# First layer: lower words of the weights made on VectorE in one operation, sums added from PSUM by VectorE, and GpSimd's paired operations merged

## The chip, the cores and the metric

The kernel runs on one core of a Trainium2 chip. The metric is the device time of one execution in microseconds (us), median of three runs. In the rows, PE is TensorE's matmuls, PEld its weight loads, DVE is VectorE, ACT is ScalarE, POOL is GpSimd and SP is SyncE, which issues the transfers.

## The reference

Eight batches of 576 tokens with 8 heads of 64 go through an attention over 32 memory slots per head, and the result (4608 tokens of width 512) goes through two feed-forward layers of width 2048. All is float32; the weights are drawn as float64 and reach the kernel as pairs of 32-bit words.

```python
a = np.exp(phi - np.max(phi, axis=2, keepdims=True))        # per head: 32 slots
a = a / (np.sum(a, axis=2, keepdims=True) + 1e-09)
k_m = np.einsum('bhsm,bhsd->bhmd', a, k)
v_m = np.einsum('bhsm,bhsd->bhmd', a, v)
scores = np.matmul(q, k_m.transpose(0, 1, 3, 2)) / np.sqrt(64)
attn = softmax(scores)                                      # over the 32 slots
x = np.matmul(attn, v_m)                                    # -> 4608 x 512
h = x @ moe_w_in;  x = np.where(h > 0, h, np.exp(np.minimum(h, 0)) - 1) @ moe_w_out
h = x @ moe2_w_in; return (h * np.clip(h + 3, 0, 6) / 6) @ moe2_w_out
```

## The kernel before, in words

Precision is kept by splitting every operand of a large product into a high part `hi` that the matrix engine takes exactly and a rest `lo`; each product is three matmuls (hi hi, hi lo, lo hi).

**First layer.** The tokens are 16 units of 288 (`T`). The attention's second product is folded into the weights `w_in` (`fold`, tiles `pw` and `wf`), so that PE makes the hidden values of one unit and one chunk of 128 hidden channels straight from the attention weights `ahi`/`alo`: this is `first(n)`, six matmuls into the PSUM tile `ph`. `middle(n)` turns `ph` into `e` and then into `g` (high and low): two operations on ACT (L671, L673), one on DVE (L675), a cast on ACT (L680) and the subtraction that leaves the low part on POOL (L682). `second(n)` multiplies `g` with the chunk of `w_out` into four PSUM tiles `acc0` to `acc3`, twelve matmuls (L706). There are 256 such items n. The first four units are worked in four quarters of the hidden channels (q = 0 to 3; quarter, then unit, then chunk), so that the weights can be made while they are used; the sums of a quarter are kept in SBUF tiles `st`, and after each later quarter `leave` adds the new sums to them. 16 blocks of four items end so, 12 of them with an addition. The other twelve units run through all 16 chunks at once.

**The weights.** `convert` makes float32 weights from the two 32-bit words of a float64. `raw` holds both words. From the upper word come the float without the lowest bits (L284 on ACT, L289, L291, L294 on DVE) and its power of two (L297 on DVE, into the place of the upper word). The lower word is scaled by 2^-52 on ACT (L287), multiplied with that power of two on POOL (L310, one operation for each chunk of 512) and added on DVE (L312). A piece is a pair of chunks, 128 x 1024; the first two pairs are worked in halves of 512. For `w_out` (`how` is "parts") a cast on ACT (L317) and a subtraction on POOL (L321) follow and give the `w1o` tiles. For the second layer's weights (`how` is "seven") the scaling and the multiplication are one DVE operation already (L300), and L303 is the addition. 16 pairs belong to the first layer, 16 to the second.

**Order.** All instructions stand in an order that a planner writes down when the program is built: each piece of work is a generator that yields a `Piece` with an engine, an estimated cost, what it needs and which buffers it takes; lanes of pieces compete by due times, and the engines' queues are filled in the planned order. Each engine then works its queue strictly in that order and waits where something is not ready. The estimated costs thus decide only the order; `early=READ` makes a piece compete as if it were due 12 items sooner.

**Second layer.** From about 720 us on, five blocks of tokens go through a scheme of seven products each; the change does not touch it.

Of the kernel before, what the change touches and what calls it, by code (L numbers as in the profile page):

```python
# [21 lines left out]
P = 128  # L22
T = 288
# [74 lines left out]
class Schedule:  # L98
# [17 lines left out]
    def mark(self, *key):  # L116
        self.done[key] = self.end

    def give(self, name, n=1):
        self.slots[name] += [self.end] * n  # L120
# [60 lines left out]
def mixer(ctx, tc, phi_t, phi_n, kv, q_t, w1i, w1o, w2i, w2o, out):  # L181
# [25 lines left out]
    def new(kind, shape, name, dt=F32):  # L207

        return pools[kind].tile(shape, dt, tag=kind, name=name)
# [34 lines left out]
    def drop(n, c):  # L244

        dropped[n] = dropped.get(n, 0) + c.stop - c.start
        if dropped[n] == 2:
            give("blk" if n in INTO else "raw")
            if n in INTO:
                give("pair")  # L250
# [14 lines left out]
    def convert(n, c, name, i, f, how, *keys):  # L265
# [19 lines left out]
        if how != "seven":  # L285
            yield Piece("act", 0.2 + 0.43 * m)
            act.activation(out=rest, in_=low, func=ACTF.Copy, scale=2.0 ** -52)  # L287
# [9 lines left out]
        dve.tensor_scalar(high, topu, 0xFF800000, None, op0=ALU.bitwise_and)  # L297
        if how == "seven":
            yield Piece("dve", two)
            dve.scalar_tensor_tensor(out=rest, in0=low, scalar=2.0 ** -52, in1=highf,  # L300
                                     op0=ALU.mult, op1=ALU.mult)
            yield Piece("dve", two)
            dve.tensor_tensor(out=top, in0=top, in1=rest, op=ALU.add)  # L303
            drop(n, c)
            tops[name, (i * FQ + f) // 2] = top
            mark("top", name, (i * FQ + f) // 2)
            return
        for x in range(m):
            yield Piece("pool", 1.2)
            pool.tensor_tensor(out=rest[:, x], in0=rest[:, x], in1=highf[:, x], op=ALU.mult)  # L310
        yield Piece("dve", two)
        dve.tensor_tensor(out=top, in0=top, in1=rest, op=ALU.add)  # L312
        drop(n, c)
        if how == "parts":
            yield Piece("act", 0.2 + 0.43 * m, **made(name, i, f, 2))
            hi, lo = make(name, i, f, m, "hl")
            act.copy(hi, top)  # L317
        for x in range(m):
            if how == "parts":
                yield Piece("pool", 1.4)  # L320
                pool.tensor_tensor(out=lo[:, x], in0=top[:, x], in1=hi[:, x].bitcast(F32),  # L321
                                   op=ALU.subtract)
            mark(name, i, f + x)
# [236 lines left out]
    def softmax(b, hf, pss, a):  # L560
# [31 lines left out]
        act.copy(a[0], zt)  # L592
        for g in range(NG):
            yield Piece("pool", 0.85)
            pool.tensor_tensor(out=a[1][:, g], in0=zt[:, g], in1=a[0][:, g].bitcast(F32),  # L595
                               op=ALU.subtract)
            mark("a", b, hf, g)
# [90 lines left out]
    def second(n):  # L688
# [4 lines left out]
        keys = [("acc", count - 1, i) for i in range(2)] if begin and count else []  # L693
# [9 lines left out]
        if close:  # L703
            passes.sort(key=lambda p: p[0])
# [11 lines left out]
    def leave(n, u, part, acc, count, i):  # L716

        key = ("second", n) if i == 0 or part else ("st", count)
        first, last = part in (None, 0), part in (None, NQ - 1)
        kind = "xy"[u >= YST]  # L720
        for d in range(i, KD, 2):
            slots = (kind, kind, "ta"[u >= YST], "ta"[u >= YST]) if (
                first and (i, d) == (0, 0)) else ()
            if not first and i == 0:
                slots = ("e",)
            engine = "act" if i == 0 or part == 0 else "dve"
            yield Piece(engine, 0.36, key, slots=slots)
            if kind in slots:
                sums2[u] = [new(kind, [P, 2, T], "st") for _ in range(2)]
                mark("st", count)  # L730
                mark("sums", u)
            st = sums2[u][d // 2][:, d % 2]
            if first and engine == "dve":
                dve.tensor_copy(st, acc[d])
            elif first:
                act.copy(st, acc[d])
            elif i:
                dve.tensor_tensor(out=st, in0=st, in1=acc[d], op=ALU.add)
            else:
                e = new("e", [P, T], "e")  # L740
                act.copy(e, acc[d])
                adds.add(add(st, d, e, count), due=n + 8)
            if n == n2 - 1:
                give(f"acc{d}")
        mark("acc", count, i)
        if last and i == 0:
            for j in range(2):
                keys = [("acc", count, 0), ("acc", count, 1)]
                if part:
                    keys += [("add", count, 2 * j)]  # L750
                leave2.add(finish(u, j, keys), due=n)

    def add(st, d, e, count):
        yield Piece("pool", 0.75)
        pool.tensor_tensor(out=st, in0=st, in1=e, op=ALU.add)
        give("e")
        mark("add", count, d)
# [268 lines left out]
    adds, leave2 = sch.lane(), sch.lane()  # L1026
# [174 lines left out]
```

## Time and profile before

| | |
|---|---|
| median of three runs | 1463.32 us (1461.45 to 1464.34) |
| the profiled execution | 1463.72 us |
| its span, first to last instruction | 1461.9 us |
| PE busy | 1414.6 us (97%) |
| DVE busy | 1095.0 us (75%) |
| ACT busy | 817.2 us (56%) |
| POOL busy | 458.8 us (31%) |

The span and the profiled execution's own time differ by 1.8 us, which lie before the first and after the last instruction. Busy shares over the whole span mix stages: POOL's 31% is nearly all in the first 700 us. An instruction counts as busy from its start to its end, so what it waits inside for a memory port is in its duration.

### The profile page before, as it was taken

The numbers are of one execution on the slowest core, as the hardware profiler recorded it, in microseconds if no ns is written. First come the engines' busy times: TensorE is split into PE (matmuls) and PEld (weight loads), VectorE is DVE, ScalarE is ACT, GpSimd is POOL, SyncE is SP. The second block draws the span as 40 slices with busy tenths as digits, with TensorE's granted clock in tenths as the row PEclk, the third lists the DMA queues.
The fourth block names the chain that finished last, engine by engine and source line by source line (L and its number), as shares of the span: only waits on it lengthen the run. The fifth ranks groups of instructions, "written<-read, shape, count | busy, mean of one in ns | idle before, by whom it ended". The sixth has DMA issues, their size and how long they took to land.

```text
span 1461.9 us, 25619 instructions
## 1 busy us (share of the span) xinstructions
PE 1414.6 (97%) x9464; PEld 1283.9 (88%) x9464; DVE 1095.0 (75%) x1785; ACT 817.2 (56%) x1691; POOL 458.8 (31%) x464
## 2 busy tenths in 40 slices
PE   4698999999999999999999999999999999999999
PEld 2588898989999899999998888888888888889998
DVE  5998865677586786767357896789678867986785
ACT  4677775667667676667653454355335534553453
POOL 1678984456557565656420000000000000000000
PEclk7799999999999999999999999999999999999999
DMA  9421215336546455654336468556936783676562
GB/s 363 184 80 71 102 63 178 101 112 236 174 162 204 155 180 178 200 170 167 124 111 239 170 226 338 194 182 222 370 140 209 247 352 131 210 274 270 204 234 117
DMA packets 94221, 279.41 MB, mean 191 GB/s; under 512 B 8976, under 2 KB 50960, under 8 KB 75920
## 3 DMA queue, kind: packets, MB, share of 16 engines
q1 hardware_dynamic: 94096, 277.78, 53.5%
q8 instruction: 74, 1.21, 0.3%
q14 instruction: 51, 0.42, 0.1%
HBM read 229.51 MB, written 48.23 MB: 190 GB/s over the span
## 4 chain that ended last, share of the span: by engine, by line
PE 87%; DVE 4%; issue 3%; POOL 3%; DMA 2%; ACT 1%; SPq 0%; DVEq 0%; ACTq 0%; POOLq 0%
PE acc L706 23%; PE ph L662 5%; PE ph L663 4%; PE ph L664 4%; PE pb L859 3%; PE qb L885 3%; PE qb L886 3%; PE qb L887 3%; PE pb L858 3%; PE pb L860 3%; PE pg L859 2%; PE pa L859 2%; PE qa L885 2%; PE qa L886 2%; PE qg L885 2%
## 5 line engine op out<-in xcount | busy, mean ns | idle before, releaser
L682 POOL TENSOR_TENSOR g<-e,g 128x288 fp32r<-128x288 f32 x256 | 251.4, 988 | 234.0 <-ACT g L680 214.5
L979 ACT CAST goh<-G 128x464 fp32r<-128x464 f32 (+1 forms) x280 | 155.6, 575 | 103.1 <-PE qb L887 46.2
L675 DVE SCALAR_TENSOR_TENSOR e<-e,ph 128x288 f32<-128x288 f32 x256 | 114.4, 449 | 129.8 <-ACT e L673 113.9
L981 DVE TENSOR_TENSOR gol<-G,goh 128x464 fp32r<-128x464 f32 (+1 forms) x280 | 172.7, 636 | 34.2 <-PE qb L886 14.0
L662 PE MATMUL ph<-ahi,wf 128*128 128x288 f32 x512 | 159.3, 311 | 5.2 <-DVE e L675 4.3
L680 ACT CAST g<-e 128x288 fp32r<-128x288 f32 x256 | 109.3, 431 | 90.1 <-DVE e L675 86.0
L947 ACT ACTIVATE e<-c,three 128x464 f32<-128x464 f32 (+1 forms) x120 | 81.9, 682 | 137.6 <-DVE c L924 123.4
L671 ACT ACTIVATE e<-ph 128x288 f32<-128x288 f32 x256 | 104.8, 409 | 95.3 <-PE ph L664 82.3
L663 PE MATMUL ph<-alo,wf 128*128 128x288 f32 x512 | 152.3, 298 | 1.5 <-POOL alo L595 1.4
L664 PE MATMUL ph<-ahi,wf 128*128 128x288 f32 x512 | 152.2, 297 | 0.2 <-DVE wf L624 0.2
L662 PEld LDWEIGHTS ph<-ahi,wf 128*128 128x128 f32 x512 | 96.9, 189 | 37.5 <-issue 14.3
L673 ACT ACTIVATE e<-e 128x288 f32<-128x288 f32 x256 | 114.0, 445 | 7.5
L663 PEld LDWEIGHTS ph<-alo,wf 128*128 128x128 f32 x512 | 97.2, 190 | 2.5 <-POOL alo L595 2.5
L664 PEld LDWEIGHTS ph<-ahi,wf 128*128 128x128 f32 x512 | 97.2, 190 | 0.4 <-DVE wf L624 0.4
L706 PE MATMUL acc<-g,w1o3h 128*128 128x288 f32 x512 | 94.3, 296 | 0.0
L706 PE MATMUL acc<-g,w1o0h 128*128 128x288 f32 x512 | 91.0, 303 | 2.4 <-ACT w1o0h L317 2.4
L706 PE MATMUL acc<-g,w1o1h 128*128 128x288 f32 x512 | 90.4, 297 | 2.4 <-POOL g L682 2.4
L706 PE MATMUL acc<-g,w1o2h 128*128 128x288 f32 x512 | 90.1, 295 | 0.0
L859 PE MATMUL pb<-op,ws 128*128 128x464 f32 (+1 forms) x240 | 89.1, 371 | 0.0
L885 PE MATMUL qb<-goh,ws 128*128 128x464 f32 (+1 forms) x240 | 88.9, 370 | 0.0
L886 PE MATMUL qb<-goh,ws 128*128 128x464 f32 (+1 forms) x240 | 88.9, 370 | 0.0
L887 PE MATMUL qb<-gol,ws 128*128 128x464 f32 (+1 forms) x240 | 88.9, 370 | 0.0
(156 smaller groups left out, 3690.8 us busy)
## 6 DMA issues: line engine op xcount, KB each, us to landing
ws<-w2o SPq DMA_DIRECT2D x70, 1024.0 KB, 5.1
ws<-w2i SPq DMA_DIRECT2D x40, 1024.0 KB, 7.4
ws<-w2i SPq DMA_DIRECT2D x40, 768.0 KB, 7.9
kvc<-in_kv SPq DMA_DIRECT2D x60, 256.0 KB, 5.5
q<-in_q_t SPq DMA_DIRECT2D x32, 288.0 KB, 4.7
x2d<-st SPq DMA_DIRECT2D x32, 288.0 KB, 3.7
raw<-in_w1i SPq DMA_DIRECT2D x8, 1024.0 KB, 8.7
raw<-in_w1o SPq DMA_DIRECT2D x8, 1024.0 KB, 9.3
```

What stands on the lines that cost most here:

```text
L662: pe.matmul(ps, whi, xhi, start=begin and c == 0, stop=False)
L663: pe.matmul(ps, whi, xlo, start=False, stop=False)
L664: pe.matmul(ps, wlo, xhi, start=False, stop=close and c == len(passes) - 1)
L675: dve.scalar_tensor_tensor(out=e, in0=e, scalar=-1.0, in1=ps, op0=ALU.add, op1=ALU.max)
L682: pool.tensor_tensor(out=lo, in0=e, in1=hi.bitcast(F32), op=ALU.subtract)
L706: pe.matmul(acc[d], w[:, f % FQ, d * P:(d + 1) * P], g[x], start=first, stop=last)
L859: pe.matmul(ps, whi, xlo, start=False, stop=False, **more)
L885: pe.matmul(ps, whi, hi, start=begin and j == 0, stop=False, **more)
L886: pe.matmul(ps, wlo, hi, start=False, stop=False, **more)
L887: pe.matmul(ps, whi, lo, start=False, stop=j == NJ - 1, **more)
L979: act.copy(hi, x)
L981: dve.tensor_tensor(out=lo, in0=x, in1=hi.bitcast(F32), op=ALU.subtract)
```

## The change

In `convert`, the first layer's pairs now take the same six DVE operations as the second layer's: ACT's scaling (L287) and POOL's multiplication (L310) go, and one DVE operation that scales and multiplies comes in their place. The low part of a `w_out` pair is one POOL operation of 1024 instead of two of 512, and the low part of the attention weights one of 576 instead of two of 288. In `leave`, the sums of the later quarters are all added by DVE, straight from PSUM (before, two of the four went through a copy on ACT and an addition on POOL, L741 and L755); the two lanes take `acc0`, `acc1` and `acc2`, `acc3` in order, and these pieces compete early. In `second`, the first item of a block goes through its twelve matmuls sum by sum, and is planned as soon as the first two sums are free.

```diff
-        if how != "seven":
-            yield Piece("act", 0.2 + 0.43 * m)
-            act.activation(out=rest, in_=low, func=ACTF.Copy, scale=2.0 ** -52)
...
         dve.tensor_scalar(high, topu, 0xFF800000, None, op0=ALU.bitwise_and)
+        yield Piece("dve", two)
+        dve.scalar_tensor_tensor(out=rest, in0=low, scalar=2.0 ** -52, in1=highf, op0=ALU.mult,
+                                 op1=ALU.mult)
+        yield Piece("dve", two)
+        dve.tensor_tensor(out=top, in0=top, in1=rest, op=ALU.add)
+        drop(n, c)
...
-        for x in range(m):
-            yield Piece("pool", 1.2)
-            pool.tensor_tensor(out=rest[:, x], in0=rest[:, x], in1=highf[:, x], op=ALU.mult)
-        yield Piece("dve", two)
-        dve.tensor_tensor(out=top, in0=top, in1=rest, op=ALU.add)
-        drop(n, c)
...
             act.copy(hi, top)
+            yield Piece("pool", 0.5 + 0.9 * m)
+            pool.tensor_tensor(out=lo, in0=top, in1=hi.bitcast(F32), op=ALU.subtract)
         for x in range(m):
-            if how == "parts":
-                yield Piece("pool", 1.4)
-                pool.tensor_tensor(out=lo[:, x], in0=top[:, x], in1=hi[:, x].bitcast(F32),
-                                   op=ALU.subtract)
...
+        yield Piece("pool", 1.2)
+        pool.tensor_tensor(out=a[1], in0=zt, in1=a[0].bitcast(F32), op=ALU.subtract)
         for g in range(NG):
-            yield Piece("pool", 0.85)
-            pool.tensor_tensor(out=a[1][:, g], in0=zt[:, g], in1=a[0][:, g].bitcast(F32),
-                               op=ALU.subtract)
...
-        keys = [("acc", count - 1, i) for i in range(2)] if begin and count else []
+
+        blocks = part is not None
+        keys = [("acc", count - 1, i) for i in range(2 - blocks)] if begin and count else []
...
-        if close:
+        if close or begin and blocks:
             passes.sort(key=lambda p: p[0])
...
-        for d in range(i, KD, 2):
+        for d in (range(i, KD, 2) if first else range(2 * i, 2 * i + 2)):
...
-            engine = "act" if i == 0 or part == 0 else "dve"
-            yield Piece(engine, 0.36, key, slots=slots)
+            engine = "act" if first and (i == 0 or part == 0) else "dve"
+            yield Piece(engine, 0.36 if engine == "act" else 0.4, key, slots=slots, early=READ)
...
-            elif i:
-                dve.tensor_tensor(out=st, in0=st, in1=acc[d], op=ALU.add)
-            else:
-                e = new("e", [P, T], "e")
-                act.copy(e, acc[d])
-                adds.add(add(st, d, e, count), due=n + 8)
```

What this makes of the order is seen at three places. The lines in the changed kernel's rows are its own: L296 is the new operation, L299 the addition after it, L286 to L294 the four before; L663 is the `e` of an item, L670 its `g`, L724 an addition to `st`, L310 the low part of `w_out`.

DVE, early in the program, the first two pairs of `w_out` (`top`) between the pieces of the second batch's summary (`kvn`, `vt`); before:

```order
L527 TENSOR_SCALAR kvn<-pkv,rs 128x128
L297 TENSOR_SCALAR raw<-top 128x1024
L537 COPY vt_139<-ptr 64x128
L289 TENSOR_SCALAR top<-top 128x1024
L527 TENSOR_SCALAR kvn<-pkv,rs 128x128
L291 TENSOR_SCALAR top<-top 128x1024
L537 COPY vt_139<-ptr 64x128
L312 TENSOR_TENSOR top<-top,raw 128x1024
L294 SCALAR_TENSOR_TENSOR top<-raw,top 128x1024
L297 TENSOR_SCALAR raw<-top 128x1024
```

and now:

```order
L516 TENSOR_SCALAR kvn<-pkv,rs 128x128
L296 SCALAR_TENSOR_TENSOR raw<-raw 128x1024
L526 COPY vt_139<-ptr 64x128
L299 TENSOR_TENSOR top<-top,raw 128x1024
L516 TENSOR_SCALAR kvn<-pkv,rs 128x128
L286 TENSOR_SCALAR top<-top 128x1024
L526 COPY vt_139<-ptr 64x128
L288 TENSOR_SCALAR top<-top 128x1024
L291 SCALAR_TENSOR_TENSOR top<-raw,top 128x1024
L294 TENSOR_SCALAR raw<-top 128x1024
L296 SCALAR_TENSOR_TENSOR raw<-raw 128x1024
L299 TENSOR_TENSOR top<-top,raw 128x1024
```

Before, the addition for the first pair (L312) stood behind two steps of the second pair, which filled the time of POOL's multiplication, and the second pair's addition came later than these rows. Now a pair's new operation and its addition follow its other steps, and the second pair's addition stands in these rows too.

POOL, around the pairs of quarter 2 of `w_out`; before:

```order
L755 TENSOR_TENSOR st<-st,e 128x288 x2
L321 TENSOR_TENSOR w1o2l<-top,w1o2h 128x512 x2
L682 TENSOR_TENSOR g<-e,g 128x288 x2
L310 TENSOR_TENSOR raw<-raw 128x512 x2
L682 TENSOR_TENSOR g<-e,g 128x288 x3
L321 TENSOR_TENSOR w1o2l<-top,w1o2h 128x512 x2
L682 TENSOR_TENSOR g<-e,g 128x288 x2
L755 TENSOR_TENSOR st<-st,e 128x288 x2
L682 TENSOR_TENSOR g<-e,g 128x288
L310 TENSOR_TENSOR raw<-raw 128x512 x2
L682 TENSOR_TENSOR g<-e,g 128x288
L755 TENSOR_TENSOR st<-st,e 128x288 x2
```

and now:

```order
L670 TENSOR_TENSOR g<-e,g 128x288 x14
L310 TENSOR_TENSOR w1o2l<-top,w1o2h 128x1024
L670 TENSOR_TENSOR g<-e,g 128x288 x3
L310 TENSOR_TENSOR w1o2l<-top,w1o2h 128x1024
L670 TENSOR_TENSOR g<-e,g 128x288 x14
```

The multiplications (L310 before) and the additions (L755) are gone from POOL's queue, which is now nothing but `g` and one operation for each pair.

DVE, at the end of a block of items in the same region; before:

```order
L297 TENSOR_SCALAR raw<-top 128x1024
L289 TENSOR_SCALAR top<-top 128x1024
L675 SCALAR_TENSOR_TENSOR e<-e,ph 128x288
L291 TENSOR_SCALAR top<-top 128x1024
L294 SCALAR_TENSOR_TENSOR top<-raw,top 128x1024
L738 TENSOR_TENSOR st<-st,acc_1462 128x288
L738 TENSOR_TENSOR st<-st,acc_1464 128x288
L312 TENSOR_TENSOR top<-top,raw 128x1024
```

and now:

```order
L663 SCALAR_TENSOR_TENSOR e<-e,ph 128x288 x2
L291 SCALAR_TENSOR_TENSOR top<-raw,top 128x1024
L294 TENSOR_SCALAR raw<-top 128x1024
L296 SCALAR_TENSOR_TENSOR raw<-raw 128x1024
L663 SCALAR_TENSOR_TENSOR e<-e,ph 128x288
L299 TENSOR_TENSOR top<-top,raw 128x1024
L286 TENSOR_SCALAR top<-top 128x1024
L724 TENSOR_TENSOR st<-st,acc_1437 128x288
L724 TENSOR_TENSOR st<-st,acc_1438 128x288
L724 TENSOR_TENSOR st<-st,acc_1439 128x288
L724 TENSOR_TENSOR st<-st,acc_1440 128x288
L663 SCALAR_TENSOR_TENSOR e<-e,ph 128x288
```

Four additions stand together at a block's end where there were two, and each conversion has one operation more, with the `e` of the items queued between and behind them.

## Rows read from the trace of the kernel before

**Rows 1.** Busy time of each engine by stretch, granted clock, DMA share, GB/s.

```profile
40.10:100.00 59.90, 46.88 (x393) 37.48 (x394) 57.01 (x80) 38.32 (x79) 38.10 (x30) 0.86 0.32 123
100.00:184.00 84.00, 75.34 (x565) 70.47 (x563) 72.97 (x87) 61.55 (x131) 78.61 (x64) 0.98 0.24 85
184.00:240.00 56.00, 55.65 (x513) 50.99 (x506) 35.47 (x63) 37.99 (x90) 38.16 (x40) 1.00 0.25 81
240.00:640.00 400.00, 399.04 (x3489) 371.49 (x3488) 282.53 (x452) 273.24 (x628) 238.70 (x253) 1.00 0.52 175
```

**Rows 2.** Waits of PE, 40.1 to 184 us: total, times, longest.

```profile
PE pw L616 <- DVE w1i L312: 4.0, 4, 1.8
PE ph L662 <- DVE e L675: 3.7, 6, 1.0
...
PE acc L706 <- POOL g L682: 2.4, 1, 2.4
```

**Rows 3.** Waits of DVE in the same stretch.

```profile
DVE e L675 <- ACT e L673: 6.8, 11, 2.0
DVE w1i L312 <- POOL raw L310: 2.4, 3, 1.3
DVE top L312 <- POOL raw L310: 1.6, 2, 1.1
```

**Rows 4.** DVE's busy time on tile w1i, then on tile top, in that stretch.

```profile
40.10:184.00 143.90, 43.36 (x30) 0.93 0.27 101
...
40.10:184.00 143.90, 38.22 (x30) 0.93 0.27 101
```

**Rows 5.** Timeline of DVE: start, duration; conversion steps while POOL rests.

```profile
39.35 0.68 DVE L312 TENSOR_TENSOR w1i<-w1i,raw 128x512 f32<-128x512 f32 x1
...
43.75 0.68 DVE L291 TENSOR_SCALAR top<-top 128x1024 uint32<-128x1024 uint32 x1
...
52.38 1.21 DVE L294 SCALAR_TENSOR_TENSOR top<-raw,top 128x1024 uint32<-128x1024 uint32 x1
```

**Rows 6.** Groups of DVE, 240 to 640 us: count, busy us, mean ns, idle before.

```profile
L303 DVE TENSOR_TENSOR top<-top,raw 128x1024 f32<-128x1024 f32 x14 | 21.1, 1506 | 0.1
L294 DVE SCALAR_TENSOR_TENSOR top<-raw,top 128x1024 uint32<-128x1024 uint32 x14 | 20.8, 1484 | 0.2
L300 DVE SCALAR_TENSOR_TENSOR raw<-raw 128x1024 f32<-128x1024 uint32 x14 | 20.5, 1466 | 0.2
L297 DVE TENSOR_SCALAR raw<-top 128x1024 uint32<-128x1024 uint32 x14 | 12.8, 913 | 0.1
L291 DVE TENSOR_SCALAR top<-top 128x1024 uint32<-128x1024 uint32 x14 | 12.6, 899 | 0.1
...
L289 DVE TENSOR_SCALAR top<-top 128x1024 f32<-128x1024 f32 x14 | 11.3, 806 | 3.4 <-ACT top L284 2.9 <-DMA w2i<-hi 0.5
```

**Rows 7.** Groups of POOL, 40.1 to 184 us.

```profile
L682 POOL TENSOR_TENSOR g<-e,g 128x288 fp32r<-128x288 f32 x41 | 50.5, 1246 | 15.7 <-ACT g L680 15.4 <-POOL g L682 0.3
L310 POOL TENSOR_TENSOR raw<-raw 128x512 f32<-128x512 f32 x24 | 29.6, 1254 | 1.3 <-DVE raw L297 1.3
L755 POOL TENSOR_TENSOR st<-st,e 128x288 f32<-128x288 f32 x11 | 12.9, 1188 | 0.0
```

**Rows 8.** Timeline of POOL: single operations that nothing lengthened.

```profile
20.53 1.04 POOL L310 TENSOR_TENSOR raw<-raw 128x512 f32<-128x512 f32 x1 [2.85 <-DVE raw L297]
...
46.66 0.80 POOL L682 TENSOR_TENSOR g<-e,g 128x288 fp32r<-128x288 f32 x1 [7.20 <-ACT g L680]
...
117.44 2.57 POOL L321 TENSOR_TENSOR w1o1l<-top,w1o1h 128x512 fp32r<-128x512 f32 x2 [0.50 <-ACT w1o1h L317]
```

**Rows 9.** Group of DVE's additions to st, 40.1 to 184 us.

```profile
L738 DVE TENSOR_TENSOR st<-st,acc 128x288 f32<-128x288 f32 x12 | 4.9, 443 | 0.1
```

**Rows 10.** Groups of ACT that go, 40.1 to 184 us.

```profile
L287 ACT ACTIVATE raw<-raw 128x1024 f32<-128x1024 uint32 x11 | 12.7, 1153 | 0.0
...
L741 ACT COPY e<-acc 128x288 f32<-128x288 f32 x12 | 4.3, 394 | 0.8 <-POOL g L682 0.8
```

More of the change, by code (lines that the diff above doesn't have):

```diff
@@ L297, in convert @@
         dve.tensor_scalar(high, topu, 0xFF800000, None, op0=ALU.bitwise_and)
-        if how == "seven":
-            yield Piece("dve", two)
-            dve.scalar_tensor_tensor(out=rest, in0=low, scalar=2.0 ** -52, in1=highf,
-                                     op0=ALU.mult, op1=ALU.mult)
-            yield Piece("dve", two)
-            dve.tensor_tensor(out=top, in0=top, in1=rest, op=ALU.add)
-            drop(n, c)
+        yield Piece("dve", two)
[4 more added lines that the diff above has]
+        drop(n, c)
+        if how == "seven":
             tops[name, (i * FQ + f) // 2] = top
@@ L307, in convert @@
             return
-        for x in range(m):
-            yield Piece("pool", 1.2)
-            pool.tensor_tensor(out=rest[:, x], in0=rest[:, x], in1=highf[:, x], op=ALU.mult)
-        yield Piece("dve", two)
-        dve.tensor_tensor(out=top, in0=top, in1=rest, op=ALU.add)
-        drop(n, c)
         if how == "parts":
@@ L716, in leave @@
     def leave(n, u, part, acc, count, i):
-        key = ("second", n) if i == 0 or part else ("st", count)
         first, last = part in (None, 0), part in (None, NQ - 1)
+        key = ("second", n) if i == 0 or part == 0 else ("st", count) if first else (
+            "acc", count, 0)
         kind = "xy"[u >= YST]
-        for d in range(i, KD, 2):
+        for d in (range(i, KD, 2) if first else range(2 * i, 2 * i + 2)):
             slots = (kind, kind, "ta"[u >= YST], "ta"[u >= YST]) if (
                 first and (i, d) == (0, 0)) else ()
-            if not first and i == 0:
-                slots = ("e",)
-            engine = "act" if i == 0 or part == 0 else "dve"
-            yield Piece(engine, 0.36, key, slots=slots)
+            engine = "act" if first and (i == 0 or part == 0) else "dve"
+            yield Piece(engine, 0.36 if engine == "act" else 0.4, key, slots=slots, early=READ)
             if kind in slots:
@@ L732, in leave @@
             st = sums2[u][d // 2][:, d % 2]
-            if first and engine == "dve":
+            if not first:
+                dve.tensor_tensor(out=st, in0=st, in1=acc[d], op=ALU.add)
+            elif engine == "dve":
                 dve.tensor_copy(st, acc[d])
-            elif first:
+            else:
                 act.copy(st, acc[d])
-            elif i:
-                dve.tensor_tensor(out=st, in0=st, in1=acc[d], op=ALU.add)
-            else:
-                e = new("e", [P, T], "e")
-                act.copy(e, acc[d])
-                adds.add(add(st, d, e, count), due=n + 8)
             if n == n2 - 1:
@@ L747, in leave @@
             for j in range(2):
[L748 to L757, printed above, removed]
+                leave2.add(finish(u, j, [("acc", count, 0), ("acc", count, 1)]), due=n)
     def finish(u, j, keys):
@@ L1025, in mixer @@
     middles = [sch.lane() for _ in range(limits["g"] + 1)]
-    adds, leave2 = sch.lane(), sch.lane()
+    leave2 = sch.lane()
     reads = {what: sch.lane() for what in ("s1", "c11", "u2", "u3", "c21", "c22", "c12")}
```

## The prediction

> **What bounds the kernel now.** I read the busy time by stretch first, because the shares over the whole span mix stages. From 240 to 640 us PE is busy 399.0 of 400 us and from 184 to 240 us 55.7 of 56: there nothing else sets the time. Before 184 us PE rests: it is busy 46.9 of 59.9 us from 40.1 to 100 and 75.3 of 84 from 100 to 184, together 122.2 of 143.9, so 21.7 us are free there [rows 1]. All that the change touches and that can move the end lies in that stretch (I come to the first 40 us below). In it DVE is busy 57.0 + 73.0 = 130.0 us (90%) and POOL 38.1 + 78.6 = 116.7 us (81%), but unevenly: to 100 us DVE has 95% and POOL 64%, from 100 to 184 us POOL has 94% and DVE 87% [rows 1]. So the first part is DVE's, and the second belongs to both.
>
> The waits say the same. PE waits longest for DVE's weights (4.0 us) and for DVE's `e` (3.7), and 2.4 us once for a `g` that stood in POOL's queue [rows 2]. DVE's own 13.9 us of rest are 6.8 for ACT's exponential, 2.4 + 1.6 = 4.0 for POOL's multiplication, and some 3 us of small pieces [rows 3]. The reader is to see that DVE has little room: what is put on it in this stretch must be paid for by what is taken off it.
>
> **DVE's conversions.** Twelve full pairs are converted from 40.1 to 184 us, with 43.36 + 38.22 = 81.6 us of DVE for 60 operations, 6.80 us a pair [rows 4]. Alone the same five take less: 0.68 for each of the three with one input and 1.21 for each of the two with two, 4.46 in all [rows 5]. The other 2.34 us a pair are DVE and POOL lengthening each other: the short durations stand where POOL rests, and POOL's too are 0.80 alone against 1246 ns in the mean for `g` [rows 7, 8].
>
> The six operations of after stand in the trace already, in the second layer's conversion: 806 + 899 + 1484 + 913 + 1466 + 1506 = 7074 ns a pair, while POOL is busy 238.7 of 400 us, 60% [rows 1, 6]. Alone they would be 4.46 + 1.21 = 5.67, so 1.40 is lengthening, at 60% of POOL.
>
> How busy will POOL be? It loses 29.6 us of multiplications and 12.9 us of additions [rows 7]: 74.2 us remain, 52%. Its `g` lose part of their own lengthening (41 x (1.246 - 0.80) = 18.3 us); if half goes, 65 us remain. The merged operations save little: 288 elements take 0.80 and 512 take 2.57 / 2 = 1.285 [rows 8], so 2.17 ns an element and 0.18 us a start, and six pairs of `w_out` halves and three of the attention's save 9 x 0.18 = 1.6 us. That makes 44 to 52%, and by proportion 1.40 x 0.44 / 0.60 to 1.40 x 0.52 / 0.60 = 1.03 to 1.21 of lengthening. I take 1.1. Bounds: 0.5, if POOL's work falls beside operations that don't mind it, and 1.40, the rate of 240 to 640 us, since POOL is less busy here than there.
>
> So a pair costs 5.67 + 1.1 = 6.77 in place of 6.80: the sixth operation is paid for by a quieter POOL. Twelve pairs: -0.4 us (-7.6 to +3.2).
>
> **DVE's other additions.** Twelve of the 24 ACT copies stand in the stretch [rows 10]; each becomes a DVE addition from PSUM at 443 ns [rows 9], a row that POOL does not lengthen: +5.3 us. Of the four half pairs at the start two come before DVE's first long wait for the attention's scores and are hidden by it; the other two take 0.68 each, as the 512-wide addition does [rows 5]: +1.4 us. If that cover is gone they cost 1.4 more.
>
> DVE: 130.0 - 0.4 + 5.3 + 1.4 = 136.3 us of 143.9 (129.1 to 139.9).
>
> **DVE's rest.** The 4.0 us behind the multiplication go, as that wait has no place left. ACT sheds 12.7 + 4.3 = 17.0 us [rows 10], and `e` no longer stands behind those copies, so I let half of the 6.8 go and keep 3.4; the 3.1 us of small pieces stay. 6.5 us (3.1 to 9.9). Stretch: 136.3 + 6.5 = 142.8, against 143.9: -1.1 us.
>
> **The merged low parts.** PE needs the first pair of `w_out` at once; half of it came after 1.285 us, the whole comes after 0.18 + 1024 x 2.17 ns = 2.40: +1.1 us once. The later pairs are made ahead of use; if they were not, it would be 1.1 for each. For the attention's low part the second half came at 1.60 and now comes at 1.43: nothing.
>
> **What stays.** In the first 40 us the chain is transfers, the first batch's attention and the fold; POOL's two early multiplications become two DVE operations of 0.68 before the same waits: nothing. The PE order of the first item of a block costs nothing by itself, for PE waits nowhere for the release of its sums now. After 184 us PE is full, and DVE (35.5 of 56 us) holds the other twelve additions, 5.3 us, and the last conversions [rows 1].
>
> **Sum.** -1.1 + 1.1 = 0. On the profiled execution's 1463.7 us that is 1463.7, and its median stands 0.4 lower: I say 1463.3. Lowest by the bounds: 129.1 + 3.1 + 1.1 = 133.3, -10.6; highest: 139.9 + 9.9 + 1.1 = 150.9, +7.0. Inside it I expect a loss to 100 us, where DVE is at 95% already, and about as much back from 100 to 184.
>
> **Weighed against the skill.** The overlap above is read as a slowing of both by some share. The page "SBUF — State Buffer" of the Trainium skill (section "SBUF: two separate sides") has it stricter: VectorE operations with two SBUF inputs or in a two-port mode and GpSimd share one port pair, an exclusive lock, and the loser blocks for the whole instruction. By that rule the pair would be held for the sum of both alone. The row that bears on it: the addition from PSUM takes 443 ns for 288 elements while POOL is busy 81% of the stretch [rows 1, 9], and the SBUF operations grow by half; that agrees with a port and does not tell sharing from a lock.
>
> **Rivals.**
>
> *Faster, POOL was the pacer.* For it: 94% from 100 to 184 us [rows 1], 4.0 us of PE's waits behind additions that waited for POOL, 2.4 behind `g` in POOL's queue [rows 2]. With these and half of the 3.7 behind `e` gone: -8.3 us, 1455. Against it: DVE gets no less work. It decides if the lengthening falls to 0.6 or less a pair and DVE's rest to some 4 us.
>
> *Much faster, one port in turn.* Held in turn, DVE's 12 x 4.46 = 53.5 and POOL's 41 x 0.80 + 24 x 1.04 + 11 x 0.80 + 12 x 1.285 + 6 x 0.80 = 86.8 us (the last two are the halves of six pairs of `w_out` and of three attention weights) make 140.3 of 143.9: full; after, 12 x 5.67 = 68.0 and 41 x 0.80 + 6 x 2.40 + 3 x 1.43 = 51.5 make 119.5 [rows 5, 7, 8]. PE's 122.2 would bound the stretch; I let three quarters of its 21.7 us of rest go: -16, 1447. This is what the lock on that page of the Trainium skill would make of it. Against it: the two engines' other work is in their queues too.
>
> *Slower, DVE is the bound throughout.* The lengthening is 1.40 as in 240 to 640 us and DVE's rest stays at 9.9: +7.0 us, 1470. Place: each block's end, where four additions (1.8 us) and a 1.2 to 1.5 us operation stand ahead of the next `e`, for which ACT's cast, POOL's `g` and PE's next item wait. It decides from 139 us of DVE in the stretch, at the rest that I keep. If the lengthening stayed at 2.34 a pair it would be 11.3 us worse than 1.40 makes it, 1481.
>
> *The change does not reach the time:* the gain of a quieter POOL sits where PE waits for the startup chain anyway. That is the forecast's time too.
>
> **Numbers.** Forecast and no effect (1459 to 1467) 0.43; faster 1455 0.23; 1447 0.06; slower 1470 0.23; 1481 0.05. What a measurement of this kernel can tell from no change is about 0.2%, 2.9 us. The forecast's case gives 0.06 of its chance to faster, 0.31 to the same and 0.06 to slower: faster 0.35, same 0.31, slower 0.34. The range, 1453 to 1472, leaves out the two far cases and the outer edge of the near ones; the forecast's own is 1459 to 1467.
>
> **What would show it.** Right: from 40 to 184 us the six operations at 6.5 to 7.0 us a pair, POOL at half of the stretch, DVE at 95%, no wait of DVE for POOL, and the `e` of the same item a few us later than before at 100 us and level at 184. Wrong to the fast side: six operations near 6.2 and PE's rest below 15 us. Wrong to the slow side: DVE without rest, seven or more a pair, and PE's waits for `e` and for the weights grown. It would be wrong altogether if the time changed after 240 us, where I see PE full.

## The result and the profile after

| | before | after |
|---|---|---|
| median, us (4 runs each) | 1463.37 (1461.45 to 1464.34) | 1479.64 (1479.28 to 1482.19) |
| span of the profiled execution, us | 1461.9 | 1480.4 |

The changed kernel is slower: ratio 1.0112, 95% interval 1.01 to 1.0124, +16.3 us. The forecast of 1463.3 us and its range up to 1472 are both missed. The profiled execution of after is the slowest of its four (1482.19 us), so what its trace has lost against before's, 18.5 us, is some 2 us more than the medians differ by.

The stretches of [rows 1], now of after (busy time and operations of PE, PEld, DVE, ACT, POOL; then the granted clock, DMA share, GB/s):

```profile
40.10:100.00 59.90, 42.53 (x324) 33.87 (x325) 52.59 (x76) 29.42 (x63) 17.62 (x13) 0.72 0.32 120
100.00:184.00 84.00, 74.28 (x532) 69.44 (x531) 77.63 (x96) 50.80 (x109) 43.79 (x33) 0.92 0.24 85
184.00:240.00 56.00, 50.99 (x412) 47.74 (x411) 43.91 (x70) 29.44 (x69) 23.81 (x21) 0.97 0.14 46
240.00:640.00 400.00, 399.95 (x3519) 370.11 (x3518) 286.59 (x461) 271.00 (x616) 227.29 (x233) 1.00 0.52 171
```

From 240 us on nothing has changed: PE is full in both. Before that the reader is to look at counts and clock rather than at busy time: PE issues 324 + 532 + 412 = 1268 matmuls to 240 us where it issued 393 + 565 + 513 = 1471, 14% fewer in 6% less busy time, since the granted clock is 0.72, 0.92 and 0.97 in place of 0.86, 0.98 and 1.00. POOL fell to 61.4 us of the stretch from 40.1 to 184, 43%, a little under the forecast's 44 to 52. DVE is busy 130.2 us there, as before, but it gets less done.

The VectorE operation that makes an item's `e` marks how far the kernel is. Counted in the trace, the one of item 8 starts 8.6 us later than before, of item 20 12.9, of item 56 19.3, and of the last, 255, 18.4. At item 56 the first layer's conversions are done. In DVE's timelines it starts at 218.2 us in before (the second of the two operations in the first row) and at 237.4 in after (the second row):

```profile
217.72 0.90 DVE L675 SCALAR_TENSOR_TENSOR e<-e,ph 128x288 f32<-128x288 f32 x2 [1.27 <-ACT e L671]
...
237.42 0.46 DVE L663 SCALAR_TENSOR_TENSOR e<-e,ph 128x288 f32<-128x288 f32 x1 [0.34 <-ACT e L661]
```

So the time is lost up to item 56 and not after it.

PE's and DVE's waits from 40.1 to 184 us, of after (total, times, longest), as in [rows 2, 3]:

```profile
PE pw L604 <- DVE w1i L299: 7.7, 2, 5.0
PE ph L650 <- DVE e L663: 7.3, 4, 2.6
PE ph L651 <- POOL alo L583: 2.8, 2, 1.8
PE acc L696 <- ACT g L668: 2.6, 1, 2.6
...
DVE wf L612 <- ACT wf L610: 4.8, 7, 1.4
DVE e L663 <- ACT e L661: 3.9, 8, 1.3
```

PE waits twice as long as before for both of DVE's products, the weights (7.7 for 4.0) and `e` (7.3 for 3.7). DVE's waits for POOL's multiplication are gone.

DVE's conversions and additions in the same stretch, of after, by group (count, busy us, mean ns, idle before):

```profile
L663 DVE SCALAR_TENSOR_TENSOR e<-e,ph 128x288 f32<-128x288 f32 x37 | 15.9, 447 | 4.8 <-ACT e L661 3.9 <-POOL g L670 0.8
L296 DVE SCALAR_TENSOR_TENSOR raw<-raw 128x1024 f32<-128x1024 uint32 x11 | 15.4, 1401 | 0.3
L288 DVE TENSOR_SCALAR top<-top 128x1024 uint32<-128x1024 uint32 x6 | 9.4, 1570 | 0.1
L291 DVE SCALAR_TENSOR_TENSOR top<-raw,top 128x1024 uint32<-128x1024 uint32 x6 | 8.9, 1485 | 0.1
L299 DVE TENSOR_TENSOR w1i<-w1i,raw 128x1024 f32<-128x1024 f32 x5 | 7.6, 1516 | 0.1
L288 DVE TENSOR_SCALAR w1i<-w1i 128x1024 uint32<-128x1024 uint32 x5 | 7.6, 1514 | 0.1
L299 DVE TENSOR_TENSOR top<-top,raw 128x1024 f32<-128x1024 f32 x6 | 7.3, 1224 | 0.1
L291 DVE SCALAR_TENSOR_TENSOR w1i<-raw,w1i 128x1024 uint32<-128x1024 uint32 x5 | 7.2, 1440 | 0.1
...
L724 DVE TENSOR_TENSOR st<-st,acc 128x288 f32<-128x288 f32 x16 | 6.3, 446 | 0.0
L294 DVE TENSOR_SCALAR raw<-top 128x1024 uint32<-128x1024 uint32 x6 | 5.4, 897 | 0.2
L286 DVE TENSOR_SCALAR top<-top 128x1024 f32<-128x1024 f32 x6 | 5.0, 833 | 0.0
L294 DVE TENSOR_SCALAR raw<-w1i 128x1024 uint32<-128x1024 uint32 x5 | 4.4, 884 | 0.1
L286 DVE TENSOR_SCALAR w1i<-w1i 128x1024 f32<-128x1024 f32 x5 | 4.0, 799 | 0.0
```

A pair of `w1i` takes 799 + 1514 + 1440 + 884 + 1401 + 1516 = 7554 ns, one of `w1o` (tile `top`) 833 + 1570 + 1485 + 897 + 1401 + 1224 = 7410; 7.48 us in the mean, where 6.77 was forecast. Below, "a pair" is always this sum of group means for 1024-wide operations, from 40.1 to 184 us; for the kernel before it is 6.84 (7266 ns for `w1i`, 6408 for `w1o`). The addition from PSUM takes 446 ns, as forecast from [rows 9].

Where the largest wait of PE comes from, in DVE's timeline of after (start, duration):

```profile
80.82 1.21 DVE L291 SCALAR_TENSOR_TENSOR w1i<-raw,w1i 128x1024 uint32<-128x1024 uint32 x1
81.95 0.83 DVE L557 STREAM_TRANSPOSE z<-ps 128x288 f32<-128x288 f32 x2
82.71 1.13 DVE L294 TENSOR_SCALAR raw<-w1i 128x1024 uint32<-128x1024 uint32 x1
83.88 1.71 DVE L296 SCALAR_TENSOR_TENSOR raw<-raw 128x1024 f32<-128x1024 uint32 x1
...
91.95 1.23 DVE L299 TENSOR_TENSOR w1i<-w1i,raw 128x1024 f32<-128x1024 f32 x1
93.09 0.81 DVE L663 SCALAR_TENSOR_TENSOR e<-e,ph 128x288 f32<-128x288 f32 x2
```

and PE behind it:

```profile
93.32 1.96 PE L604 MATMUL pw<-w1i,vt 64*32 64x512 f32 x16 [5.04 <-DVE w1i L299]
```

For 12 us DVE has little but conversion steps in its queue, the rest of one pair and the whole of the next, and no `e` runs from 80.9 to 93.1. PE has used up what it had at 88.3 and waits for the end of the second pair.

### The profile page after: what moved, and what is told of

Read it like the earlier page. It is cut to its first block, busy times and chain, and to the rows that moved or that the text cites. A ratio compares the mean times of both kernels' runs of the same rounds, so it can differ in the third digit from the quotient of the medians.

```text
span 1480.4 us, 25543 instructions
## 1 busy us (share of the span) xinstructions
PE 1423.6 (96%) x9464; PEld 1292.6 (87%) x9464; DVE 1118.2 (76%) x1827; ACT 796.1 (54%) x1649; POOL 385.8 (26%) x384
## 3 DMA queue, kind: packets, MB, share of 16 engines
q8 instruction: 74, 1.21, 0.3%
## 4 chain that ended last, share of the span: by engine, by line
PE 89%; DVE 4%; issue 1%; ACT 1%; DMA 1%; POOL 0%; DVEq 0%; ACTq 0%; POOLq 0%; SPq 0%
PE acc L696 25%; PE ph L650 5%; PE ph L652 4%; PE ph L651 4%; PE pb L836 3%; PE qb L862 3%; PE qb L863 3%; PE qb L864 3%; PE pb L835 3%; PE pb L837 3%; PE pg L836 2%; PE pa L836 2%; PE qa L862 2%; PE qa L863 2%; PE qg L862 2%; PE qg L864 2%
## 5 line engine op out<-in xcount | busy, mean ns | idle before, releaser
L670 POOL TENSOR_TENSOR g<-e,g 128x288 fp32r<-128x288 f32 x256 | 247.9, 973 | 299.3 <-ACT g L668 273.2
L663 DVE SCALAR_TENSOR_TENSOR e<-e,ph 128x288 f32<-128x288 f32 x256 | 114.1, 449 | 106.7 <-ACT e L661 90.3
L650 PEld LDWEIGHTS ph<-ahi,wf 128*128 128x128 f32 x512 | 98.4, 192 | 40.2 <-DVE e L663 15.8
L652 PEld LDWEIGHTS ph<-ahi,wf 128*128 128x128 f32 x512 | 98.8, 193 | 0.1
L696 PE MATMUL acc<-g,w1o0h 128*128 128x288 f32 x512 | 94.2, 307 | 4.8 <-ACT g L668 2.6
```

The lines of the kernel that those rows point to most:

```text
L650: pe.matmul(ps, whi, xhi, start=begin and c == 0, stop=False)
L652: pe.matmul(ps, wlo, xhi, start=False, stop=close and c == len(passes) - 1)
L663: dve.scalar_tensor_tensor(out=e, in0=e, scalar=-1.0, in1=ps, op0=ALU.add, op1=ALU.max)
L670: pool.tensor_tensor(out=lo, in0=e, in1=hi.bitcast(F32), op=ALU.subtract)
L696: pe.matmul(acc[d], w[:, f % FQ, d * P:(d + 1) * P], g[x], start=first, stop=last)
```

## The experiments

Four theories were to be told apart. **O**, order: the scheduler plans with the new costs, puts conversion steps ahead of items' work, and PE waits; the work itself is paid for. **T**, total: VectorE has more to do than fits, in any order. **K**: the merged, long GpSimd operations hold VectorE up. **D**: the additions at a block's end delay the next `e`. All runs, with how late `e` starts against before at four items; each ratio is against before as it ran beside that run (medians from 1462.97 to 1464.36 us):

| run | median us | ratio, 95% interval | item 8 | 20 | 56 | 255 |
|---|---|---|---|---|---|---|
| after | 1479.64 | 1.0112, 1.01 to 1.0124 | +8.6 | +12.9 | +19.3 | +18.4 |
| e1_conv | 1479.74 | 1.0114, 1.0099 to 1.0129 | +7.1 | +8.5 | +17.2 | +18.5 |
| e2_adds | 1459.54 | 0.9976, 0.9967 to 0.9986 | -0.4 | -0.2 | -3.5 | -4.3 |
| e3_merges | 1475.48 | 1.0081, 1.0064 to 1.0099 | +4.6 | +3.9 | +15.4 | +10.8 |
| e4_no_merges | 1476.72 | 1.0093, 1.0078 to 1.0108 | +5.9 | +5.2 | +12.1 | +12.9 |
| e8_conv_kept_order | 1473.34 | 1.0065, 1.005 to 1.008 | +5.4 | +6.1 | +9.2 | +8.5 |
| e9_merges_kept_order | 1465.8 | 1.0014, 1.0005 to 1.0024 | +0.5 | +1.4 | +1.7 | +1.1 |
| e10_all_kept_order | 1473.91 | 1.0068, 1.0053 to 1.0083 | +7.6 | +8.8 | +11.1 | +10.4 |
| e5_after_early | 1493.98 | 1.0204, 1.0187 to 1.0221 | +7.8 | +15.6 | +32.0 | +30.3 |
| e6_before_early | 1466.2 | 1.0017, 1.0007 to 1.0026 | +2.4 | -4.6 | +1.0 | +1.0 |
| e11_after_costs | 1482.09 | 1.0126, 1.0111 to 1.0142 | +8.0 | +11.4 | +20.6 | +18.9 |
| e12_before_costs | 1474.83 | 1.0075, 1.006 to 1.009 | +2.7 | +1.4 | +12.1 | +11.5 |
| e13_adds_costs | 1471.71 | 1.0053, 1.0036 to 1.0069 | +3.5 | +1.2 | +7.7 | +8.2 |
| e14_relief_alone | 1452.65 | 0.9925, 0.991 to 0.994 | -2.1 | -5.9 | -11.8 | -12.7 |
| e15_sixth_alone | 1486.91 | 1.0165, 1.0146 to 1.0185 | +6.3 | +11.1 | +23.3 | +23.3 |

### The parts alone

`e1_conv` is before with the conversion's part of the change:

```diff
-            act.activation(out=rest, in_=low, func=ACTF.Copy, scale=2.0 ** -52)
-            pool.tensor_tensor(out=rest[:, x], in0=rest[:, x], in1=highf[:, x], op=ALU.mult)
+        dve.scalar_tensor_tensor(out=rest, in0=low, scalar=2.0 ** -52, in1=highf,
+                                 op0=ALU.mult, op1=ALU.mult)
```

> The kernel before with the conversion part of the change alone (scale and multiply in one VectorE operation, nothing on ScalarE and GpSimd for it). Theory O (order): the extra VectorE operation turns the conversions into unbroken runs on VectorE of up to 12 us ahead of the items' e, TensorE waits for weights and e and falls to half clock: +10 to +16 us against before. Theory K (long GpSimd operations hold VectorE up): the merged operations carry the loss, so this alone gives +3 to +6. Theory D (additions at the block ends): 0 to +4.

`e2_adds` is before with the sums alone:

```diff
-                e = new("e", [P, T], "e")
-                act.copy(e, acc[d])
-                adds.add(add(st, d, e, count), due=n + 8)
+                dve.tensor_tensor(out=st, in0=st, in1=acc[d], op=ALU.add)
```

> The kernel before with the part on the sums alone (VectorE adds all later quarters' sums from PSUM, twelve matmuls of a block's first item sum by sum). O: 0 to +3 us, since the loss of 13 us before the first such addition (item 16) cannot come from it. K: 0. D: +4 to +8, from item 20 on.

`e3_merges` is before with the merged GpSimd operations alone (here the attention's; the weights' likewise):

```diff
-            pool.tensor_tensor(out=a[1][:, g], in0=zt[:, g], in1=a[0][:, g].bitcast(F32),
-                               op=ALU.subtract)
+        pool.tensor_tensor(out=a[1], in0=zt, in1=a[0].bitcast(F32), op=ALU.subtract)
```

> The kernel before with GpSimd's merged operations alone (one of 1024 for a w_out pair, one of 576 for the attention weights). O: -1 to +2 us. K: +5 to +10, with VectorE steps of 2 to 3 us beside a 2.4 us GpSimd operation. D: 0.

`e4_no_merges` is after with the last diff taken back:

> The changed kernel with GpSimd's operations in halves again (conversion and sums as changed). O: +12 to +17 us against before, near the changed kernel's +16. K: +6 to +10. D: +14 to +17.

Measured: +16.8, -3.4, +12.5 and +13.8 us. D falls: the additions alone make the kernel faster. By parts the loss is the conversion's, as O has it, but the merges alone cost 12.5 us, more than K's 5 to 10 and far from O's -1 to +2, and only about 3 on top of the other two. Of O, K and D, none has its ranges right in all four runs. Parts that don't add up point to something that each of them changes: the order. In the merges alone DVE's work is that of before, and yet DVE's timeline reads

```profile
134.69 0.68 DVE L289 TENSOR_SCALAR w1i<-w1i 128x1024 f32<-128x1024 f32 x1
135.41 1.42 DVE L291 TENSOR_SCALAR w1i<-w1i 128x1024 uint32<-128x1024 uint32 x1
136.86 1.95 DVE L294 SCALAR_TENSOR_TENSOR w1i<-raw,w1i 128x1024 uint32<-128x1024 uint32 x1
138.73 1.82 DVE L312 TENSOR_TENSOR w1i<-w1i,raw 128x1024 f32<-128x1024 f32 x1
...
141.80 0.81 DVE L672 SCALAR_TENSOR_TENSOR e<-e,ph 128x288 f32<-128x288 f32 x2
```

and PE's

```profile
142.30 0.40 PE L659 MATMUL ph<-ahi,wf 128*128 128x288 f32 x1 [4.29 <-DVE e L672]
```

ACT's exponentials for these two items ended at 133.7 and 135.8 us. The `e`s were ready, and stood behind conversion steps.

### The same work in the order of before

If the order is the cause, the change must be nearly free when the order stays. In `e8_conv_kept_order` the scheduler still books the pieces that are gone; they issue nothing, and the new operation is issued without a piece of its own:

```diff
             yield Piece("act", 0.2 + 0.43 * m)
-            act.activation(out=rest, in_=low, func=ACTF.Copy, scale=2.0 ** -52)
...
             yield Piece("pool", 1.2)
-            pool.tensor_tensor(out=rest[:, x], in0=rest[:, x], in1=highf[:, x], op=ALU.mult)
         yield Piece("dve", two)
+        dve.scalar_tensor_tensor(out=rest, in0=low, scalar=2.0 ** -52, in1=highf,
+                                 op0=ALU.mult, op1=ALU.mult)
```

> The conversion part alone, as in the run that cost 16.8 us, but planned as before: the scheduler still books the ACT copy and the two GpSimd multiplications, only that nothing is issued there, and the one VectorE operation is issued just ahead of the final addition without a booking of its own. So VectorE carries all the added operations of the first layer, and the order of the rows on TensorE, ScalarE and VectorE is that of before but for these. Theory O (what costs is the new order that the planner writes): most of the 16.8 us goes, 1458 to 1468 us. Theory T (VectorE has more to do before 184 us than fits, in any order): 1474 to 1482 us stay.

`e9_merges_kept_order` does the same for the merges (`if g == 0:` ahead of the whole operation, both bookings kept):

> The merged GpSimd operations alone, as in the run that cost 12.5 us, but planned as before: both halves are still booked, the whole operation is issued at the first booking. The order of the rows on TensorE, ScalarE and VectorE is that of before, word for word. Theory O: within 3 us of before, 1460 to 1466. Theory K (a long GpSimd operation holds VectorE up, whatever the order): 1470 to 1476, as with the planner's new order.

`e10_all_kept_order` has all three parts, in the order planned for `e2_adds`:

> All the work of the changed kernel in the order that was planned for the additions alone (the version at 1459.5 us): the sixth VectorE operation and the merged GpSimd operations are issued, but the planner still books the ACT copy, the two multiplications and the halves, as in the two runs with the order kept. If the costs of the work itself add up, -3.4 + 9.5 + 2.0 gives +8.1 us, 1472 us, and the other 8 us of the changed kernel are its order (theories T for the first half and O for the second). T alone: 1478 to 1482. O alone: 1460 to 1466.

Measured +9.5, +2.0 and +10.3 us. The merges are settled: 2 us are theirs and the other 10.5 were the order's; K is worth 2 us. The conversion is split: 7.3 us of its 16.8 go with the order, but 9.5 stay though every other row stands where it stood. Neither O nor T had that: 1473.3 us lies 5 above O's range and 0.7 below T's. All three parts come to 1473.9, where the sum of the parts gave 1472. The stretches of `e8_conv_kept_order`:

```profile
40.10:100.00 59.90, 41.20 (x340) 32.28 (x340) 55.43 (x78) 30.02 (x65) 21.48 (x19) 0.83 0.32 123
100.00:184.00 84.00, 76.85 (x576) 72.54 (x576) 75.60 (x93) 55.31 (x123) 56.40 (x48) 0.98 0.24 85
184.00:240.00 56.00, 51.34 (x472) 46.28 (x471) 37.84 (x61) 33.88 (x81) 33.23 (x36) 1.00 0.19 59
240.00:640.00 400.00, 399.91 (x3478) 372.05 (x3473) 284.26 (x454) 274.43 (x629) 237.89 (x252) 1.00 0.52 172
```

DVE is busy 131.0 of the 143.9 us to 184 us and rests 12.9, a little less than before (13.9, [rows 1]), and a pair takes 7.54 us (8121 ns for `w1i`, 6970 for `w1o`), 0.70 more than before. The first layer has 14 full pairs: 14 x 0.70 = 9.8 us. The four single conversions at the start have a sixth operation too, 0.68 each; what of these 2.7 us is hidden there, the run doesn't show.

### The two terms of the pair

The sixth operation and the relief by a quieter POOL, each by itself in the order of before. `e14_relief_alone` leaves POOL's multiplication out with nothing in its place, and with it a part of the computation; `e15_sixth_alone` has a sixth VectorE operation beside all of before's work.

> The kernel before in its own order, with GpSimd's multiplications of the first layer left out and nothing in their place (the lower words then stay unmultiplied, so this part of the computation is missing). It prices the relief alone. The prediction's step: a conversion of five operations falls from 6.80 to some 5.4 us a pair, 12 pairs, -17 us or less where PE then bounds, 1447 to 1455. Theory T, with each operation's lengthening in proportion to GpSimd's share of the stretch: 0.45 x 0.63 / 0.81 = 0.35 us for each of five operations, 6.2 us a pair, -6 us, 1456 to 1460.

```diff
-            pool.tensor_tensor(out=rest[:, x], in0=rest[:, x], in1=highf[:, x], op=ALU.mult)
```

> The kernel before in its own order and with all its work, and one more VectorE operation of two SBUF inputs in each conversion of the first layer, just ahead of the final addition; it leaves its data as they are. It prices the sixth operation alone, with GpSimd as busy as before. Theory T: 1.21 us alone and 0.45 of lengthening, 12 pairs, +20 us, 1480 to 1486. Theory O: +3 to +10, 1466 to 1473, since the order is kept. If the relief of the other run and this price add up to about the +9.5 us of the conversion part in the kept order, both terms are the cause.

```diff
         yield Piece("dve", two)
+        dve.scalar_tensor_tensor(out=rest, in0=rest, scalar=1.0, in1=rest, op0=ALU.mult,
+                                 op1=ALU.max)
```

The stretches of `e14_relief_alone` to 240 us:

```profile
40.10:100.00 59.90, 48.44 (x396) 39.14 (x397) 56.22 (x81) 40.04 (x84) 27.73 (x24) 0.89 0.32 121
100.00:184.00 84.00, 81.74 (x642) 77.27 (x641) 70.26 (x98) 69.47 (x147) 59.37 (x55) 1.00 0.26 89
184.00:240.00 56.00, 55.66 (x510) 51.08 (x509) 30.92 (x58) 34.59 (x86) 30.74 (x36) 1.00 0.40 132
```

and of `e15_sixth_alone`:

```profile
40.10:100.00 59.90, 41.93 (x339) 33.48 (x338) 56.17 (x75) 32.73 (x66) 30.80 (x25) 0.89 0.30 111
100.00:184.00 84.00, 68.99 (x499) 63.42 (x499) 72.79 (x85) 54.97 (x116) 68.22 (x54) 0.96 0.25 91
184.00:240.00 56.00, 50.07 (x400) 46.39 (x400) 45.43 (x60) 36.81 (x83) 49.34 (x42) 0.97 0.12 37
```

Measured -11.7 and +22.5 us; together +10.8, against +9.5 for both in one kernel. The relief brings a pair to 5.83 us, 1.01 less; 14 of them are 14.1 us, and it gains 11.7, PE being busy 81.7 of 84 us from 100 to 184 then. The sixth operation brings a pair to 8.24, 1.40 more, 19.6 us for 14; the four single conversions, 0.68 each, make it 22.3. So the time follows DVE's work about one for one, to within some 3 us. In pairs the two don't add up so well: -1.01 + 1.40 is +0.39, and with both in one kernel it was +0.70; POOL's share of the stretch differs too (61% in `e14`, 69% in `e15`, 54% in `e8`). The relief stands midway: 5.83 us a pair where the prediction's step says 5.4 and T 6.2; the time lies in the range given for the prediction's step, but that range reached so far only because it allowed for PE becoming the bound. The price of the sixth operation is T's (1486.9 us, 0.9 above its range), and about what the prediction's own numbers leave for it, 1.40 for 6.77 - 5.4 = 1.37: what the prediction had wrong is how little a quieter POOL takes off the operations.

### Other orders of the same work

In `e5_after_early` and `e6_before_early` the `e` goes ahead of conversion steps, in after and in before:

```diff
-        yield Piece("dve", 0.4)
+        yield Piece("dve", 0.4, early=READ)
         dve.scalar_tensor_tensor(out=e, in0=e, scalar=-1.0, in1=ps, op0=ALU.add, op1=ALU.max)
```

> The changed kernel with one word more: the VectorE operation that makes an item's e is planned as 12 items more urgent than its due time, so that it is put ahead of conversion steps whenever ACT's exponential is planned to be ready. The work of every engine stays. Theory O: the time that a ready e stands behind VectorE's earlier operations, 141 us summed over the first 52 items, falls to 90 or less, TensorE's waits for e go, and 8 to 16 of the 16.3 us come back: 1464 to 1472. Theory T: 1476 to 1484, the conversions become late in place of the e's.

> Control: the same word in the kernel before. Theory O: 0 to 5 us less than before, since TensorE's waits for e are 3.7 us there; if it gains as much as in the changed kernel, the urgency of e is worth something by itself and does not explain the difference of the two. Theory T: within 3 us of before.

In the other three only numbers of the planner change, nearer to measured durations (here those of `e12_before_costs`):

```diff
-        one, two = ((0.65, 0.75), (0.95, 1.35))[m - 1]
+        one, two = ((0.65, 0.75), (1.15, 1.65))[m - 1]
...
-        yield Piece("pool", 0.85)
+        yield Piece("pool", 1.25)
```

> The changed kernel with other numbers in the planner and no other work: a pair's VectorE operations are booked at 1.05 and 1.45 us in place of 0.95 and 1.35, GpSimd's low part of g at 1.1 in place of 0.85, nearer to what they took in its trace. Theory O: the order alone moves the time by 4 us or more, and with truer numbers rather down, 1468 to 1476. Theory T: 1477 to 1482.

> Control: the same numbers of the planner in the kernel before, set to what its own trace shows (1.15, 1.65, and 1.25 for g). Its work is unchanged. Theory O: the order by itself moves the time by several us, up or down: anywhere from 1455 to 1475, and a plan nearer to the measured durations rather down. Theory T: within 3 us of before, since the work of every engine is the same.

> The additions alone (1459.5 us) with the planner's numbers of the control, 1.15, 1.65 and 1.25. Theory O: several us up or down, from 1452 to 1472. Theory T: within 3 us of 1459.5.

Measured against their own bases: +14.3 (`e5` on after), +2.4 (`e6` on before), +2.5 (`e11` on after), +11.2 (`e12` on before), +12.2 (`e13` on the additions alone). Five new orders of unchanged work, none faster; the 2.5 us of `e11` lie within the spread of its runs and after's. What I expected of `e5` was wrong in its sign, and `e11` and `e12`, planned with truer numbers, went up where I expected them rather down. Summed over the first 52 items, the time that a ready `e` stands before DVE takes it falls from 141 us in after (89 in before) to 18 in `e5`, and the kernel is 14 us slower: the conversions and the attention's pieces come late in its place. From 40.1 to 240 us PE waits there 6.9 us for a step of the attention's summary (`nb`), 4.7 for the attention's low part, and 4.1 and 3.8 for the two parts of a `w_out` pair (`w1o2`). A late `e` is a sign of a bad order, and not by itself its price. In `e12_before_costs`, to 184 us,

```profile
40.10:184.00 143.90, 123.46 (x890) 108.64 (x887) 117.64 (x156) 97.40 (x198) 102.45 (x88) 0.86 0.28 101
```

DVE is busy 117.6 us where it was 130.0 [rows 1], and rests 26.3: from 40.1 to 240 us it waits

```profile
DVE e L675 <- ACT e L673: 29.5, 20, 6.7
DVE e L675 <- POOL g L682: 6.5, 3, 4.7
```

for the items' own chain (before 19.5 us for the first of these), at a granted clock of 0.86 to 184 us for 0.93. An order can lose time with DVE idle as well as with DVE full.

## Why the prediction was wrong

**The stretch and the engine: right.** All that moved the time lies before the first layer's conversions end, and DVE sets the pace there. Work on DVE and time change about one for one in `e8` (9.8 us of work, 9.5 of time), `e14` (14.1 and 11.7) and `e15` (22.3 and 22.5). That is the rival "DVE is the bound throughout", given 0.23 and 1470 us; its place, the additions at a block's end, was wrong (`e2_adds` is faster). The far rival of 1481 us comes nearest to the measured time, but by luck: it has the lengthening stay at 2.34 us a pair, and it is 1.81, while 6 us of the loss are the order, which no rival had.

**The conversions: the step that failed.** The prediction has a pair at "5.67 + 1.1 = 6.77 in place of 6.80". It took the lengthening from the second layer, 1.40 at a POOL 60% busy [rows 1, 6], and cut it to 1.1, with 1.40 as upper bound. Measured it is 7.48 - 5.67 = 1.81 in after, at a POOL 43% busy, and 7.54 - 5.67 = 1.87 in the kept order, at 54%. The stretch's own row said so: 2.34 for five operations at 81% is 0.47 each; at 52%, by proportion, 0.30, and for six 1.80, 7.47 a pair. It was the nearer row, and was left for a farther one. That it meets the measured 7.48 so closely is chance: at the 43% that POOL is busy in after the same proportion gives 7.15. So the sixth operation is not paid for by a quieter POOL: +0.70 a pair in the kept order. Of the prediction's signs for the slow side, seven or more a pair and PE's grown waits came; DVE without rest did not.

**Twelve pairs.** The stretch was cut at 184 us because PE is full from there before. But the conversions behind that point are paid too once PE has to wait for them: in after PE is busy 51.0 of 56 us from 184 to 240. It is 14 full pairs and 4 singles. 0.70 x 14 = 9.8, where the prediction had -0.4; `e8_conv_kept_order` lost 9.5. The additions were cut at 184 us too: counted in the trace, DVE makes 36 of them before item 56 in after and 18 in before, so 18 more, 8.0 us at 446 ns, where the prediction had 5.3.

**DVE's rest.** "6.5 us" by 184 us; it is 7.3 + 6.4 = 13.7 in after and 13.9 before. The two waits it was made of did go as forecast: POOL's multiplication wholly, and ACT's exponential to 3.9 (3.4 forecast). But waits that had been next to nothing took their place, above all 4.8 us for ACT's part of the fold (0.3 before). So DVE's rest was no reserve that this edit could spend; it moved to the next wait.

**The order.** The prediction priced work and took the order as it comes. All three parts in a kept order cost 10.3 us, the changed kernel, with the same instructions in another order, 16.3: 6 us are the order that the planner drew from the new costs, with runs of conversion steps like the one at 80.8 us. How these 6 split into waits and clock, no run told apart. Nor did the three parts' prices add up exactly, -3.4 + 9.5 + 2.0 = 8.1 against 10.3.

**The small terms.** The addition at 443 ns: 446. Merged low parts, 1.1 us: 2.0 (0.7 to 3.5 by its interval). That the lock held in turn would free 16 us: not seen, though the lock itself was (below).

The additions alone (`e2_adds`) are faster than both kernels, 1459.5 us. POOL is relieved of its additions there (a pair falls to 6.32, 14 x 0.52 = 7.3 us), but DVE has the 18 additions more, 8.0 us; so this balance does not explain the gain. It has an order of its own too, and what the gain comes from is not shown.

## What to carry to other kernels

When an operation moves to an engine that is 90% busy, price it with the lengthening of its own stretch, and count every instance that the waiting engine will come to need, not those within a window of the old trace. Where a scheduler draws the order, an edit changes two things; keep the old bookings once and issue the new work in them, and the work's price stands apart from the order's. Here five redrawn orders of unchanged work cost 2 to 14 us, at most nearly as much as the change itself.

## What the runs showed of the hardware

**One operation held for a whole other one.** In after a conversion step of one input, 0.68 us alone [rows 5], in DVE's timeline:

```profile
55.77 2.75 DVE L288 TENSOR_SCALAR top<-top 128x1024 uint32<-128x1024 uint32 x1
```

and POOL's beside it:

```profile
55.62 2.35 POOL L310 TENSOR_TENSOR w1o0l<-top,w1o0h 128x1024 fp32r<-128x1024 f32 x1 [11.00 <-ACT w1o0h L308]
```

POOL ends at 57.97, DVE 0.55 us later, a little less than its time alone; POOL, first to start, took no longer than the 2.40 expected of it alone. That is holding, not sharing, and it is no single case. Counted in the trace of after from 40.1 to 240 us, all 17 one-input 128x1024 operations of DVE that start inside a POOL operation with more than 0.3 us of it left end 0.55 us behind POOL's end, and 16 of the 17 with two inputs end 1.08 us behind it (1.21 to 1.23 alone). The other way round, 23 of the 25 `g` operations that start inside a 128x1024 operation of DVE with more than 0.2 us of it left end 0.65 to 0.67 us behind DVE's end (0.80 alone). The Trainium skill's page "SBUF — State Buffer", section "SBUF: two separate sides", says so of the shared port pair (an exclusive lock for the whole instruction), and these rows agree. What the prediction made of that rule, two busy times that only add up, does not follow: a DVE operation that starts inside a POOL operation waits for what is left of it, and 0.3 us an operation remain at a POOL half busy. Nor does the lengthening go in proportion to POOL's share of the stretch: it is 0.47 us an operation at 81% (before), 0.43 at 69% (`e15`), 0.27 at 61% (`e14`), 0.31 at 54% (`e8`) and 0.30 at 43% (after). Operations with an operand in PSUM keep their time: `e` 447 ns in after and 445 in before, the additions 446 and 443.

**The clock falls in PE's waits.** In after the granted clock is 0.72 from 40.1 to 100 us. The longest stretch at 1.2 of 2.4 GHz there begins at 41.2 us (20.5 us long), inside a wait of PE of 2.62 us for weights that ends at 42.4; another begins at 92.4, inside the 5.04 us wait shown above.
